# Attention with two problems in one kernel: two heads ahead of the first scores, fewer products in some slots of B, another order of the first loads, a start by quarters, and no branch hint on SyncE

## The chip, the cores and the metric

The kernel runs on one core of a Trainium2 chip. The metric is device time in microseconds (us) of that core. A kernel is run several times, and medians are quoted. Runs are sorted by state: one run of the kernel before took 396.01 us at a granted clock of 0.853 and counts as slow; all others are fast, and only fast runs are compared.

## The reference, cut to what matters

Two independent problems, A and B, of the same form; the outputs stand side by side.

```python
B, Sq, D = 16, 32, 1024
Hq, Hkv, Sk, Dh = 32, 4, 512, 128
q = (x @ wq).reshape(B, Sq, Hq, Dh).transpose(0, 2, 1, 3)
k = jnp.repeat(k_cache, 8, axis=1)
v = jnp.repeat(v_cache, 8, axis=1)
scores = jnp.einsum("bhqd,bhkd->bhqk", q, k) * (Dh ** -0.5)
p = softmax(scores)
o = jnp.einsum("bhqk,bhkd->bhqd", p, v)
out = o.transpose(0, 2, 1, 3).reshape(B, Sq, Hq * Dh) @ wo
# result: concatenate([out_A, out_B], axis=-1), all bfloat16
```

## The kernel before

TensorE (PE in the profile) has three kinds of work: query products (512 tokens at a time, 8 products per head), scores and values of one (batch row, group) pair, and output products. A slot handles one pair: four score products of 256 columns, four value products of the pair five slots earlier, and 6 or 7 "units" taken from one long stream of query and output products of 512 columns. The stream fills PE while ScalarE (ACT) does the exponential and VectorE (DVE) the sums and the normalization. There are 64 slots of A, then 64 of B.

```python
def stream():
    for h in range(REP, HQ):        # REP = 8: heads 8 to 31 of A
        yield from q_units(0, h)
    for h in range(HQ):
        yield from q_units(1, h)
    ...                             # output products of A, then of B
units = stream()
run(units, DC)                      # DC = 8: one head ahead of the first scores
...
for i in range(total_slots + LAG):  # 128 + 5
    if live:
        do_loads(i)
        scores(i)
    run(units, 1)
    ...                             # sums of a group of four slots
    if i >= LAG:
        values(i - LAG)
    ...                             # reciprocals, spread, normalize on DVE
    run(units, 5)
    if live:
        partial_sums(i)
    run(units, 1 - (i % 4 == 3))
```

The first eight heads are a special part. x and the weights arrive in pieces, x is transposed on PE, and dummy products (`warm_up`) keep PE busy meanwhile:

```python
load_x(0, 0, TT // 2)               # all of these loads are issued by SyncE
load_w0(0, 1, 0, NF // 2)
load_x(0, TT // 2, TT)
load_w0(0, 1, NF // 2, NF)
load_w0(1, 2, 0, NF)                # "second row block": weights of rows 128 to 255
load_x(2, 0, TT)
...
load_wq(0, 2, 0, 2)                 # third weight block, first half (heads 8, 9)
load_k(0)
load_wq(0, 2, 2, 4)                 # second half (heads 10, 11)
load_wq(0, 3)
load_k(1)
load_v(0)
load_k(2)
load_wq(0, 4)
load_v(1)
...
warm_up(22)
transpose_x(0, 0, TT // 2)          # two 128-row blocks of x, first half of the tokens
warm_up(3)
first_heads((0, 1), (0,), 0, TT // 2)
transpose_x(0, TT // 2, TT)
first_heads((2,), (0,), 0, TT // 2)
warm_up(1)
first_heads((0, 1, 2), (0,), TT // 2, TT)
first_heads((3, 4, 5), (0,), 0, TT // 2)
first_heads((3, 4, 5), (0,), TT // 2, TT)
first_heads(range(0, NF - 2), (1,)) # the first products of 512 columns
```

At the very end every engine branches over a fallback path that is not taken in these runs. A hint for this branch is given to all five engines. The call stands near the end of the source; in the trace the hints run before the engine's own work, at 0.70 to 0.82 us.

## Time and profile before

| | |
|---|---|
| time before, first three runs | 343.67 us median (343.37 to 343.81) |
| span of the profiled run | 342.1 us (its time: 343.89) |
| PE busy | 338.1 us, 99% |
| first PE instruction, last product starts | 0.93 us, 338.74 us |

These are lines of the page of the kernel before. The first gives the span. The second gives busy time, share and instructions by engine. The third is the chain of work that ended last, by engine. The last two are groups of weight loads (PEld), of the later heads' weights (wq_sb) and of the first heads' (w_sb): after the bars each has busy time and mean, then idle time before it and what ended that.

```profile
span 342.1 us, 5510 instructions
...
PE 338.1 (99%) x2128; PEld 214.6 (63%) x2128; DVE 265.6 (78%) x336; ACT 185.7 (54%) x209; POOL 46.6 (14%) x206
...
PE 99%; ACT 0%; issue 0%; ACTq 0%
...
L301 PEld LDWEIGHTS <-wq_sb 128*128 128x128 bf16 x448 | 43.8, 98 | 31.7 <-DMA wq_sb<-in_A_wq_dram 0.2
...
L533 PEld LDWEIGHTS <-w_sb 128*128 128x128 bf16 x70 | 7.2, 104 | 6.9
```

PE is the whole chain, but busy time of overlapping matmuls doesn't show whether they follow each other as fast as they can. The start-to-start distance of neighbours does. In the instruction records of this run, after 6.5 us, a 512-column product is followed after 216 ns and a 256-column product after 109 ns, whatever comes next. The longest distance is 240 ns, once. So PE never stalls after 6.5 us, and only what lies before can be shortened, apart from the fixed tail after the last product (3.36 us).

This is the timeline of the start of the kernel before: start and length in us, engine, line, operation, output and inputs, count. SPq is SyncE's issue of a DMA.

```profile
0.86 0.45 SPq L465 DMA_DIRECT2D x_sb<-in_A_x_dram  x1
...
0.93 2.52 PE L515 MATMUL q_ps<-const-bfloat16-1.0 128*128 128x128 bf16 x22 [0.93 <-PEq L695]
...
3.29 0.61 PE L523 MATMUL xT_ps<-ident,x_sb 128*128 128x128 bf16 x4
...
3.69 0.53 PE L515 MATMUL q_ps<-const-bfloat16-1.0 128*128 128x128 bf16 x3
...
4.07 0.59 PE L533 MATMUL q_ps<-xT,w_sb 128*128 128x256 bf16 x2
...
5.25 2.58 PE L533 MATMUL q_ps<-xT,w_sb 128*128 128x256 bf16 x13
```

The 22 dummies take 107 ns each, and the 256-column products from 5.41 us on follow each other every 213 ns. At 6.47 us this falls to 110 ns. So PE runs at half rate until then (213 against 110 ns; for 128 columns 107 before and 56 after); I call that moment the switch.

### The profile page before, as it was taken

The page shows a single profiled execution, that of the slowest core. Times are in us where ns is not written, and L with a number is a line of the kernel's source. Part 1 is how long each engine was busy: PE and PEld are TensorE (multiplying, and loading weights), DVE is VectorE, ACT ScalarE, POOL GpSimd, SP SyncE. Part 2 cuts the span into 40 slices and gives each one's busy share as a digit, 9 for nine tenths or more (in the row PEclk, how much of TensorE's full clock was granted, in tenths as well). Part 3 has the DMA queues.
Part 4 walks back from the last instruction along what each step waited for, and adds up shares of the span by engine and source line. Part 5 has one row for each costly group of instructions (what it writes and reads, how often), then busy time and mean ns, then how long its engine had stood idle before and what let it go on. Part 6 is the DMA issues. An engine that isn't in the chain of part 4 may idle for free.

```text
span 342.1 us, 5510 instructions
## 1 busy us (share of the span) xinstructions
PE 338.1 (99%) x2128; PEld 214.6 (63%) x2128; DVE 265.6 (78%) x336; ACT 185.7 (54%) x209; POOL 46.6 (14%) x206
## 2 busy tenths in 40 slices
PE   8999999999999999999999999999999999999996
PEld 7456666666666666666666666666666666666555
DVE  1047988888888889888888888798888888889540
ACT  2067666676666666676655554555454555555110
POOL 0001111101111111111101212222122100111100
DMA  6999999899999998999999856999439996430001
GB/s 194 253 243 183 284 261 256 173 232 269 299 234 248 238 252 231 251 304 303 281 319 259 191 125 180 283 323 211 129 104 306 350 194 139 103 96 17 17 17 33
DMA packets 128093, 71.70 MB, mean 210 GB/s; under 512 B 75840, under 2 KB 127296, under 8 KB 128064
## 3 DMA queue, kind: packets, MB, share of 16 engines
q1 hardware_dynamic: 127536, 70.21, 84.7%
q0 software_dynamic: 384, 1.05, 0.9%
q8 instruction: 17, 0.28, 0.3%
q14 instruction: 12, 0.10, 0.1%
q10 hardware_dynamic: 144, 0.07, 0.1%
HBM read 50.86 MB, written 2.10 MB: 155 GB/s over the span
## 4 chain that ended last, share of the span: by engine, by line
PE 99%; ACT 0%; issue 0%; ACTq 0%
PE f_ps L320 32%; PE q_ps L301 28%; PE ob L425 16%; PE s_ps L357 16%; PE q_ps L533 4%; PE q_ps L515 1%; PE xT_ps L523 0%; ACT o_sb L329 0%; ACTq L329 0%
## 5 line engine op out<-in xcount | busy, mean ns | idle before, releaser
L365 ACT ACTIVATE p_sb<-s_ps,shift 128x1024 bf16<-128x1024 f32 x128 | 142.6, 1114 | 97.8 <-PE s_ps L357 82.0
L376 DVE TRANSPOSE_TENSOR_REDUCE parts<-p_sb 128x32 f32<-128x1024 bf16 x128 | 158.8, 1240 | 19.2 <-ACT p_sb L365 17.6
L320 PE MATMUL f_ps<-wo_sb,oT 128*128 128x512 bf16 (+1 forms) x544 | 131.8, 366 | 0.0
L301 PE MATMUL q_ps<-xT,wq_sb 128*128 128x512 bf16 x448 | 117.4, 379 | 0.0
L425 PE MATMUL ob<-p_sb,v_sb 128*128 128x256 bf16 x512 | 76.8, 273 | 0.0
L357 PE MATMUL s_ps<-qT,kT 128*128 128x256 bf16 x512 | 76.8, 273 | 0.0
L320 PEld LDWEIGHTS <-oT 128*128 128x128 bf16 x544 | 53.2, 98 | 35.8
L357 PEld LDWEIGHTS <-kT 128*128 128x128 bf16 x512 | 56.9, 113 | 28.3
L301 PEld LDWEIGHTS <-wq_sb 128*128 128x128 bf16 x448 | 43.8, 98 | 31.7 <-DMA wq_sb<-in_A_wq_dram 0.2
L425 PEld LDWEIGHTS <-v_sb 128*128 128x128 bf16 x512 | 50.1, 98 | 20.0
L447 DVE TENSOR_TENSOR oT<-r,ob 128x512 bf16<-128x512 f32 x64 | 43.9, 686 | 21.9 <-PE ob L425 20.8
L411 DVE STREAM_TRANSPOSE r<-rall 128x512 f32<-128x512 f32 x64 | 44.2, 691 | 1.1
L309 ACT CAST qT<-q_ps 128x512 bf16<-128x512 f32 x56 | 32.6, 583 | 15.4 <-PE q_ps L301 15.4
L394 POOL COPY half<-cs 64x32 f32<-64x32 f32 x32 | 6.5, 204 | 227.4 <-DVE cs L384 227.3
L329 ACT CAST o_sb<-f_ps 128x512 bf16<-128x512 f32 (+1 forms) x17 | 9.5, 558 | 24.6 <-PE f_ps L320 24.6
L533 PE MATMUL q_ps<-xT,w_sb 128*128 128x512 bf16 (+1 forms) x70 | 15.4, 377 | 0.0
L384 DVE TENSOR_REDUCE cs<-parts 128x32 f32<-128x128 f32 x32 | 12.0, 376 | 1.1
L406 DVE RECIPROCAL rall<-sums 128x32 f32<-128x32 f32 x32 | 10.2, 320 | 3.3 <-POOL sums L403 3.3
L533 PEld LDWEIGHTS <-w_sb 128*128 128x128 bf16 x70 | 7.2, 104 | 6.9
L561 DVE CAST qT<-q_ps 128x512 bf16<-128x512 f32 x4 | 2.5, 683 | 10.2 <-PE q_ps L533 10.2
L331 POOL DMA_DIRECT2D out_dram<-o_sb x8 | 4.6, 574 | 34.7 <-ACT o_sb L329 34.6
L395 POOL TENSOR_TENSOR half<-half,cs 64x32 f32<-64x32 f32 x32 | 7.8, 242 | 2.6
(25 smaller groups left out, 46.3 us busy)
## 6 DMA issues: line engine op xcount, KB each, us to landing
v_sb<-in_A_v_cache_dram SPq DMA_DIRECT2D x16, 512.0 KB, 6.5
wq_sb<-in_B_wq_dram SPq DMA_DIRECT2D x8, 1024.0 KB, 6.0
wo_sb<-in_A_wo_dram SPq DMA_DIRECT2D x8, 1024.0 KB, 6.4
v_sb<-in_B_v_cache_dram SPq DMA_DIRECT2D x16, 512.0 KB, 4.4
wo_sb<-in_B_wo_dram SPq DMA_DIRECT2D x8, 1024.0 KB, 8.4
wq_sb<-in_A_wq_dram SPq DMA_DIRECT2D x5, 1024.0 KB, 6.3
wq_sb<-in_A_wq_dram SPq DMA_DIRECT2D x2, 512.0 KB, 5.8
kT<-in_A_k_cache_dram SPq DMA_TRANSPOSE x64, 4.5
```

The lines of the kernel that those rows point to most:

```text
L301: nc.tensor.matmul(ps[:], lhsT=w[:, dc, (h % 4) * DH:(h % 4 + 1) * DH], rhs=xT[pr][:, dc, :], start=(dc == 0), stop=(dc == DC - 1),)
L309: nc.scalar.copy(out=qT[pr, g][:, :, hl, :], in_=ps[:].rearrange("p (b s) -> p b s", s=SQ),)
L320: nc.tensor.matmul(ps[:, 0:width], lhsT=oT[pr, tt][:, h, :], rhs=wo_tiles[pr, nh, h // REP][:, h % REP, off:off + width], start=(h == 0), ...
L357: nc.tensor.matmul(s_ps[:, c, :], lhsT=kT[:, i % GRP, c, :], rhs=qT[pr, g][:, b, :, :].rearrange("p h s -> p (h s)"), start=True, stop=True,)
L365: nc.scalar.activation(out=p_sb[:], in_=s_ps[:], func=ACTF.Exp, bias=shift[:], scale=SCALE)
L376: nc.vector.tensor_reduce(out=parts[k][:, q, :, :].rearrange("p c h -> p (c h)"), in_=st[i]["p"][:].rearrange("p c (h s) -> p (c h) s", s=SQ),
L384: nc.vector.tensor_reduce(out=cs[:], in_=parts.pop(k)[:].rearrange("p q c h -> p q h c"), axis=AX.X, op=ALU.add,)
L406: nc.vector.reciprocal(out=rall[:, k, :], in_=quad.pop(k)[:])
L411: nc.vector.transpose(out=r[:].rearrange("p n s -> p (n s)"), in_=rall[:, k, o * 2 * REP:(o + 1) * 2 * REP] .unsqueeze(2).to_broadcast([P, ...
L425: nc.tensor.matmul(ob[j][:, q, :], lhsT=v_sb[:, i % GRP, c, :], rhs=st[i]["p"][:, c, :], start=(c == 0), stop=(c == KC - 1),)
L447: nc.vector.tensor_tensor(out=out, in0=rcp.pop(j)[:].rearrange("p (q h) s -> p q h s", h=REP), in1=ob.pop(j)[:].rearrange("p q (h s) -> p ...
L533: nc.tensor.matmul(first_q[h][:, ts], lhsT=w0[dc // HC][:, dc % HC, h * DH:(h + 1) * DH], rhs=xT[0][:, dc, ts], start=(dc == 0 and t0 == 0 ...
```

## The change

Its intent, read from the code: the first real product should come sooner (transpose and copy 128 tokens instead of 256 before it, one dummy less, first DMA issued sooner without SyncE's hint). The first scores and the weights of heads 10 and 11 should have more time to wait for their loads (eight more products ahead of the scores, third weight block whole before K, later weight blocks a slot sooner). The slots of B give the eight products back, so that the tail stays as long. The diff, cut to its core:

```diff
             load_wq(0, 2, 0, 2)
+            load_wq(0, 2, 2, 4)
             load_k(0)
-            load_wq(0, 2, 2, 4)
             load_wq(0, 3)
             load_k(1)
             load_v(0)
+            load_wq(0, 4)
             load_k(2)
-            load_wq(0, 4)
             load_v(1)
 ...
             warm_up(22)
-            transpose_x(0, 0, TT // 2)
-            warm_up(3)
-            first_heads((0, 1), (0,), 0, TT // 2)
-            transpose_x(0, TT // 2, TT)
-            first_heads((2,), (0,), 0, TT // 2)
+            for tt in range(2):
+                transpose_x(0, tt, tt + 1, nc.vector.tensor_copy)
+            transpose_x(1, 0, 2, nc.scalar.copy, spare)
+            warm_up(2)
+            first_heads((0, 1, 2), (0,), 0, 1)
+            transpose_x(0, 2, TT, nc.vector.tensor_copy)
+            transpose_x(1, 2, TT, nc.scalar.copy)
+            first_heads((0, 1, 2), (0,), 1, 2)
             warm_up(1)
 ...            # transpose_x now does one row block; `spare` is one more PSUM buffer
-            run(units, DC)
+            run(units, 2 * DC)
 ...
-                need = ((c4 - 2) * 4 - 1) * DC / 6.75
+                need = ((c4 - 2) * 4 - 2) * DC / 6.75
                 at(max(0, int(need) - 7), load_wq, c4 // 8, c4 % 8)
 ...
-                run(units, 1 - (i % 4 == 3))
+                run(units, i % 4 != 3 and (i < NG or i % 8 != 1))
 ...
-                [nc.sync.engine, nc.scalar.engine, nc.vector.engine, nc.tensor.engine, nc.gpsimd.engine],
+                [nc.scalar.engine, nc.vector.engine, nc.tensor.engine, nc.gpsimd.engine],
```

More of the change, by code (lines that the diff above doesn't have):

```diff
@@ L510, in fast_path @@
                 first_q += [pair_ps[:, k, :] for k in range(2)]
+            spare = psum.tile([P, NTOK], BF16, name="xT_ps", tag="proj")
             first_q += [psum.tile([P, NW], FP32, name="q_ps", tag="proj")[:] for _ in range(2)]
@@ L515, in warm_up, with transpose_x @@
                     nc.tensor.matmul(
-                        first_q[NF - 1][:, 0:P], lhsT=warm, rhs=warm, start=True, stop=True
+                        first_q[HALF][:, 0:P], lhsT=warm, rhs=warm, start=True, stop=True
                     )
-            def transpose_x(d0, t0, t1):
-                for d, copy in ((d0, nc.vector.tensor_copy), (d0 + 1, nc.scalar.copy)):
+            def transpose_x(d, t0, t1, copy, ps=None):
+                if ps is None:
                     ps = psum.tile([P, NTOK], BF16, name="xT_ps", tag="ob")
-                    for tt in range(t0, t1):
-                        nc.tensor.transpose(
-                            ps[:, tt * P:(tt + 1) * P], x_sb[:, tt, d * P:(d + 1) * P], ident[:]
-                        )
-                    ts = slice(t0 * P, t1 * P)
-                    copy(out=xT[0][:, d, ts], in_=ps[:, ts])
+                for tt in range(t0, t1):
+                    nc.tensor.transpose(
+                        ps[:, tt * P:(tt + 1) * P], x_sb[:, tt, d * P:(d + 1) * P], ident[:]
+                    )
+                ts = slice(t0 * P, t1 * P)
+                copy(out=xT[0][:, d, ts], in_=ps[:, ts])
             def first_heads(heads, dcs, t0=0, t1=TT):
@@ L541, in fast_path @@
             warm_up(22)
-            transpose_x(0, 0, TT // 2)
-            warm_up(3)
-            first_heads((0, 1), (0,), 0, TT // 2)
-            transpose_x(0, TT // 2, TT)
-            first_heads((2,), (0,), 0, TT // 2)
+            for tt in range(2):
[6 more added lines that the diff above has]
+            first_heads((0, 1, 2), (0,), 1, 2)
             warm_up(1)
-            first_heads((0, 1, 2), (0,), TT // 2, TT)
-            first_heads((3, 4, 5), (0,), 0, TT // 2)
-            first_heads((3, 4, 5), (0,), TT // 2, TT)
+            first_heads((0, 1, 2), (0,), 2, TT)
+            first_heads((3, 4, 5), (0,), 0, 2)
+            first_heads((3, 4, 5), (0,), 2, TT)
             first_heads(range(0, NF - 2), (1,))
-            transpose_x(2, 0, TT)
+            transpose_x(2, 0, TT, nc.vector.tensor_copy)
+            transpose_x(3, 0, TT, nc.scalar.copy)
             first_heads(range(NF - 2, NF), (1,))
```

## The prediction

> **What bounds the kernel.** TensorE, almost without a gap. The page has PE busy 338.1 of 342.1 us (99%), and the chain of waits that ended last is 99% PE. By start-to-start distances in the instruction records: after about 6.5 us 512-column products follow each other every 216 ns and 256-column ones every 109 ns, whatever comes between, with no longer gap up to the end (the longest is 240 ns, once). The 92 products after the last values are as dense. The list of waits names PE once, 0.9 us, before its first instruction; one wait of a weight load for a DMA (0.2 us) stayed hidden. Reordering the steady part can win nothing.
>
> What is not dense is the ends: 0.93 us before PE starts, then 22 dummy products, then a slow clock. Until 6.47 us the distances are 107 ns for 128 columns and 213 ns for 256; then 110 for 256. [...] the trace agrees with the two rates (107 and 56 ns for 128 columns), and places the switch 5.5 us after PE's first instruction. The last 2.5 us are the last copy and output DMA.
>
> **What the change does.**
> 1. Start: one dummy less (107 ns at the slow clock), the first token half transposed, copied and multiplied by quarters. The first real product waited until 4.07 us; a 128-column copy should be done by about 3.80 us (256-column copies took 0.29, 512-column 0.42, so I estimate 0.22) and the two dummies end at about 3.88, so no wait. Counting 39 slow steps of 107 ns instead of 40, and waits of together about 0.08 us gone, the products of the second token half start near 5.06 instead of 5.25 us. If the clock switches at the same moment, that 0.19 us is worth half afterwards: about 0.1 us.
> 2. No hint on SyncE: its hint took 60 ns plus issue, so the first DMA issues about 0.08 us earlier (0.86 before). x landed at 3.24, just when PE wanted it. At the end its branch may take longer, but it has from 336.4 to 341.1 us to spare.
> 3. Two heads ahead (8 more products before the first scores, so these come near 23.0 instead of 21.3 us), whole third weight block before K: K's first slice lands about 3 us later (18.0 before) but is wanted 1.7 later: still about 2 us early. The block's second half (landed 23.15, wanted about 23.3) and the fifth block (38.3, wanted about 38) gain 2 to 3 us of margin. PE did not stall there before: safety, not time.
> 4. Nine products fewer in slots of B: it balances the eight ahead; the tail has 93 instead of 92. VectorE needs about 8.4 us per four slots against 9.1 us in the shortened groups: still room.
>
> PE's work in columns is the same but for the dummy. Sum: 343.67 - 0.1, perhaps 0.2 with earlier data. I predict **343.5 us**, 343.0 to 344.0. Faster by over 2%: 0.5%; within 2%: 99%; slower: 0.5%.
>
> **In the profile:** first scores near 23.0 us; distances unchanged at 216/109 ns; the second token half's first product near 5.06 us; slow clock until about 6.5 us; the last matmul at about 338.9; no new PE waits.
>
> **What would make it wrong:** [...] a stall at K or V because the transposing DMAs come later; VectorE falling behind in the shortened slots; SyncE's unhinted branch outlasting the last output.

Two passages are cut out because no trace or run shows them: where the half rate comes from, with how long it lasts and how much it scatters, and the first of the risks, that the clock switches at another moment, with a size for it. "The two rates" are the measured 107 and 56 ns that stand beside them. 343.67 less 0.1 is 343.57, less 0.2 is 343.47, so 343.5.

## The result, and the profile after

| | median us | range | runs |
|---|---|---|---|
| before | 343.56 | 343.37 to 343.95 | 6 |
| after | 343.33 | 343.06 to 343.81 | 6 |

The ratio is 0.9993, with a 95% interval of 0.998 to 1.0006. A ratio is the mean time of one kernel's fast runs over that of the other's of the same rounds, so it is not quite the ratio of the medians quoted. The measured time lies within the predicted range. The times alone don't show that the change helps at all, since the interval contains 1. The traces do, and they show something that I had not predicted.

The page of the changed kernel, the same lines:

```profile
span 341.5 us, 5512 instructions
...
PE 337.4 (99%) x2130; PEld 214.4 (63%) x2130; DVE 265.6 (78%) x337; ACT 185.8 (54%) x209; POOL 46.7 (14%) x206
...
PE 99%; ACT 0%; issue 0%; ACTq 0%
...
L301 PEld LDWEIGHTS <-wq_sb 128*128 128x128 bf16 x448 | 43.8, 98 | 32.2
...
L534 PEld LDWEIGHTS <-w_sb 128*128 128x128 bf16 x73 | 7.1, 102 | 6.8 <-DMA w_sb<-in_A_wq_dram 0.3
```

And the timeline of its start:

```profile
0.74 0.45 SPq L465 DMA_DIRECT2D x_sb<-in_A_x_dram  x1
...
3.24 0.63 PE L524 MATMUL xT_ps<-ident,x_sb 128*128 128x128 bf16 x4
...
3.67 0.42 PE L516 MATMUL q_ps<-const-bfloat16-1.0 128*128 128x128 bf16 x2
...
3.88 0.53 PE L534 MATMUL q_ps<-xT,w_sb 128*128 128x128 bf16 x3
...
5.00 2.19 PE L534 MATMUL q_ps<-xT,w_sb 128*128 128x256 bf16 x13
...
6.15 0.55 PEld L534 LDWEIGHTS <-w_sb 128*128 128x128 bf16 x4 [0.28 <-DMA w_sb<-in_A_wq_dram]
...
22.60 0.60 PE L357 MATMUL s_ps<-qT,kT 128*128 128x256 bf16 x4
```

The first DMA is issued 0.12 us sooner (0.74 for 0.86). The first real product starts at 3.88 instead of 4.07 us. But the span fell by 0.64 us, three times what these could give, and a new wait stands at 6.15 us. The switch explains both. Here the trace has a record of the granted clock, which rises at 4.89 us, where the run before switched at 6.47. With the faster clock, PE reached the products of the second row block ("first wide product" below: 512 columns) before their weights had landed (6.10 us). The distance to the first of them was 277 instead of 109 ns, a wait of 0.17 us. So two profiled runs with two different switches cannot tell what the change did. The experiments must hold the switch apart from the change.

### The profile page after: what moved, and what is told of

It reads as the page before. It is cut to its first block, busy times and chain, and to the rows that moved or that the text cites. A ratio compares the mean times of both kernels' runs of the same rounds, so it can differ in the third digit from the quotient of the medians.

```text
span 341.5 us, 5512 instructions
## 1 busy us (share of the span) xinstructions
PE 337.4 (99%) x2130; PEld 214.4 (63%) x2130; DVE 265.6 (78%) x337; ACT 185.8 (54%) x209; POOL 46.7 (14%) x206
## 4 chain that ended last, share of the span: by engine, by line
PE 99%; ACT 0%; issue 0%; ACTq 0%
PE f_ps L320 32%; PE q_ps L301 28%; PE ob L425 16%; PE s_ps L357 16%; PE q_ps L534 4%; PE q_ps L516 1%; PE xT_ps L524 0%; ACT o_sb L329 0%; ACTq L329 0%
## 5 line engine op out<-in xcount | busy, mean ns | idle before, releaser
L534 PE MATMUL q_ps<-xT,w_sb 128*128 128x512 bf16 (+2 forms) x73 | 14.9, 359 | 0.0
```

The lines of the kernel that those rows point to most:

```text
L534: nc.tensor.matmul(first_q[h][:, ts], lhsT=w0[dc // HC][:, dc % HC, h * DH:(h + 1) * DH], rhs=xT[0][:, dc, ts], start=(dc == 0 and t0 == 0 ...
```

## The experiments

Theory A: the steady part takes the same time in both kernels; the moment of the switch is chance; the change gains about 0.1 us in the start. Rivals: the change itself brings the switch forward (B), the gain comes from the new order (C), or the dummies don't matter to the switch (D). Unless the edit says otherwise, the base is the changed kernel. All twelve runs gave correct results. Each call has its own runs of the kernel before on the same chip: their medians were 343.54 us in the first call (343.52 without its slow run) with the repeat, the start alone, the order alone and no dummies, 343.87 in the second (the two delayed kernels, no compensation, two queues), 343.58 in the third (no hint, 20 dummies, one load on ScalarE) and 343.74 in the last (hint back). In some traces some 40 of 2130 PE records are missing; a distance of twice the usual length with nothing named as waited for is such a hole, not a stall.

### The same kernel again

No edit.

> The changed kernel, unaltered. The two profiles differ by 0.64 us in span (342.10 and 341.47), but the TensorE clock switched at 6.47 us in the one before and at 4.89 us in the one after. Theory A (the moment of the switch is chance, each us of it is worth half a us, the change itself is worth 0.1 us): over the repeats the spans scatter over 0.5 us or more, and a profile that switches later is longer by half the delay, apart from 0.17 us of DMA wait that only the early switch shows. Rival B (the change itself brings the switch forward, or shortens the steady part): every repeat switches near 4.9 us and has a span of 341.4 to 341.5. Median 343.2 to 343.6 under A, 343.2 to 343.3 under B.

Measured: 343.33 us (343.08 to 343.95), ratio 0.9993 (0.9977 to 1.0008). The profiled run switched at 5.53 us, not 4.89, and its span was 341.58 us. So the kernel doesn't fix the switch, and B as stated falls. Whether the start shifts the odds of an early switch is taken up below the table at the end. The six times fall into two groups: four from 343.08 to 343.37, two at 343.93 and 343.95.

### The start alone, and the order alone

The first is the kernel before with the new first part (quarters, two dummies) and without SyncE's hint. The second is the kernel before with the other hunks (loads, `2 * DC`, `need`, slots of B).

> The kernel before with the quartered start and without the SyncE hint; order and slots of before. Theory A (all of the gain lies in the start): the median is 0.1 to 0.2 us under that of before, the first product of the second token half near 5.0 us, distances of 216 and 109 ns afterwards. Rival C (the gain comes from the new order of products and loads): as before within 0.05 us. The difference is near the noise, so the trace decides: 39 slow steps in place of 40 and no waits before 5.0 us.

> The kernel before with only the order changed: two heads ahead, fewer products in the slots of B, third weight block whole before K, weight loads a slot sooner; start and SyncE hint of before. Theory A: PE was gapless there, so no change: median within 0.1 us of before, start distances as before, first scores near 23 us. Rival C: 0.2 us or more faster.

Measured: the start alone 343.50 us (343.21 to 344.62), the order alone 343.78 (343.40 to 344.10), before in the same call 343.54. Ratios to before: 0.9991 (0.9977 to 1.0005) and 0.9998 (0.9985 to 1.0012). None is clear of 1. By the medians theory A missed in both: the start alone is 0.02 to 0.04 us under before, not 0.1 to 0.2, which is what C expected, and the order alone is 0.24 to 0.26 above, not within 0.1 (C, which wanted it 0.2 faster, missed there). The expectation had left the decision to the trace. Of the runs, the start alone has its fastest at 343.21, 343.22 and 343.25; the six fastest of before lie at 343.46 to 343.54. The order alone has its fastest at 343.40. That comparison was chosen after the runs; it speaks for A and against C, and so do the traces: the order alone keeps the old start distances and takes as long from its first wide product to its last product as the kernel before (331.94 us).

In the trace of the start alone, the distances up to 5.05 us are 107 ns throughout. The first product of the second token half starts there (5.05), as in the repeat, against 5.25 in the kernel before. But its profiled run was its slowest, 344.62 us. The list of its weight loads' waits (us in total, times, longest) says why:

```profile
PEld L301 <- DMA wq_sb<-in_A_wq_dram: 0.9, 2, 0.6
...
PEld L534 <- DMA w_sb<-in_A_wq_dram: 0.6, 1, 0.6
PEld L425 <- DMA v_sb<-in_A_v_cache_dram: 0.5, 1, 0.5
```

With the old order the second half of the third weight block landed at 24.34 us in this run (23.15 in the kernel before's profile) and PE stood: the distance at 23.77 us is 620 instead of 216 ns, so 0.40 us were lost, 0.32 at the first values that need the second load of V (41.1 us), 0.28 at row-block weights (7.9 us). The last of these stalls has nothing to do with the change of order, since both kernels issue those loads in the same order. The other 0.72 us show that the old order can stall without any added delay; this is the one trace that shows it.

### Does the order buy margin?

To both kernels, one load of 256 KB that nothing reads was added, so that what follows lands later:

```diff
             load_wq(0, 2, 0, 2)
+            extra = blk_tile([P, REP * DH], "extra")
+            nc.sync.dma_start(out=extra[:], in_=wq_v[:, 0, 0:REP * DH])
```

> The kernel before with one more load, 256 KB that nothing reads, right behind the first half of the third weight block, so that everything behind it lands about 1.0 to 1.5 us later (an estimate from the 3.1 us that 512 KB took there). Theory E (the new order buys margin at the third weight block, not time): in the kernel before, the second half of the block landed at 23.15 us and was wanted at about 23.2, so nearly all of the delay becomes a wait of PE: 0.8 to 1.6 us longer than before, seen as a wait of the weight load near 23.3 us. Rival F (margins are ample in both orders, the order is worth nothing): within 0.2 us of before.

> The changed kernel with the same extra 256 KB load in the same place. Theory E: the third block landed at 19.1 us and its second half is wanted near 22.9, the first slice of K at 19.6 and is wanted at 22.4, the fourth block at 26.1 and is wanted near 27.4; a delay of 1.0 to 1.5 us uses this up but no more: 0 to 0.3 us longer than the changed kernel, so 343.2 to 343.7 us, and about 1 us faster than the other kernel with the same load. Rival F: both kernels with the load differ by no more than 0.2 us.

Measured in one call: 344.81 us (344.02 to 345.30) for the old order and 343.88 (343.71 to 344.24) for the new one; before without the load 343.87. Ratios to before: 1.002 (1.0001 to 1.0039) and 0.9998 (0.9981 to 1.0015). The difference of the two medians is 0.93 us, as theory E expected. Not all of it is the order, since the two kernels differ in the start too: in the profiled runs the first wide product starts at 6.92 and 6.60 us, and the time from there to the last product differs by 0.82 us (332.76 and 331.94). The new order landed somewhat above the range I gave it (343.2 to 343.7); the reason comes below. The waits of the weight loads, first the old order:

```profile
PEld L517 <- issue: 0.9, 1, 0.9
PEld L301 <- DMA wq_sb<-in_A_wq_dram: 0.8, 1, 0.8
PEld L425 <- DMA v_sb<-in_A_v_cache_dram: 0.4, 1, 0.4
```

and the new order, which has none for a DMA:

```profile
PEld L518 <- issue: 0.9, 1, 0.9
```

In the old order the half block landed at 24.80 us, and PE's distances of 829 and 400 ns (216 undisturbed) make 0.80 us of stall. In the new order it landed at 20.10 us. So margin is what the order buys, about 0.8 us under this delay, shown by a delay made on purpose.

Both kernels of this pair pay something else, equally. Their tails, from the last product's start to the end, are 3.79 us instead of 3.36. In the records of the changed kernel, the DMAs of SyncE and ScalarE take semaphores 102 to 109 in turn, and at the end SyncE waits for these eight in the same order; those that it finds done follow each other after 0.06 us (336.21, 336.27, 336.33, 336.39, 336.45 us for 102 to 106). The last output has 109 and landed at 340.49; the wait for it, at 340.51, is the last. In the delayed new order, with one DMA more, seven more waits follow the last output's landing (340.95 to 341.37 us). It is the same in both, so the comparison holds, but it explains most of why the delayed new order is above the changed kernel (0.43 of 0.55 us, between two calls).

### The dummies

```diff
-            warm_up(22)
...
-            warm_up(2)
...
-            warm_up(1)
```

> The changed kernel with all 25 dummy products taken out. Theory A ([...] the dummies buy an early switch): PE starts near 3.05 us when x lands instead of 0.93; the real products start some 0.2 us earlier, but the switch comes about 2 us later, so the median is 0.5 to 1.2 us longer than that of the changed kernel and the switch lies between 6.5 and 9 us. Rival D (the switch comes at a fixed time after launch whatever PE does): the switch stays between 4.9 and 6.5 us and the kernel is as fast or 0.1 to 0.2 us faster.

Measured: 344.66 us (344.09 to 344.96), against 343.33 for the changed kernel in the same call: 1.33 longer, a little more than expected; ratio to before 1.0025 (1.001 to 1.0041). PE started at 2.95 us and the switch came at 8.07, beyond every switch seen with dummies and an undisturbed start (3.77 to 6.73). D falls: dummies buy an earlier switch. PE's wait list shows the idle start:

```profile
PE xT_ps L524 <- DMA x_sb<-in_A_x_dram: 2.9, 1, 2.9
```

### The slots of B without the compensation

```diff
-                run(units, i % 4 != 3 and (i < NG or i % 8 != 1))
+                run(units, i % 4 != 3)
```

> The changed kernel without the nine products fewer in the slots of B. Theory A (PE is gapless, so where its products stand does not matter): same as the changed kernel within 0.1 us; the last values come some 2 us earlier and the tail has 9 products fewer (84 in place of 93). Rival G (the thinner slots of B are needed, because VectorE or a PSUM buffer falls behind, or the thinner slots themselves cost): 0.3 us or more slower or faster, with waits or longer distances in B.

Measured: 344.28 us (344.05 to 344.81), ratio to before 1.0011 (0.9994 to 1.0028), before in the same call 343.87. Theory A failed in this expectation, and so did my sign: the last values come later (327.23 us against 324.53), as the products that were in the tail now stand ahead of them. This is the timeline near the end:

```profile
323.24 0.38 PE L320 MATMUL f_ps<-wo_sb,oT 128*128 128x512 bf16 x1
323.44 0.69 DVE L447 TENSOR_TENSOR oT<-r,ob 128x512 bf16<-128x512 f32 x1 [0.63 <-PE ob L425]
...
324.19 1.47 PE L320 MATMUL f_ps<-wo_sb,oT 128*128 128x512 bf16 x6 [0.57 <-DVE oT L447]
...
327.86 0.69 DVE L447 TENSOR_TENSOR oT<-r,ob 128x512 bf16<-128x512 f32 x1 [2.99 <-PE ob L425]
...
328.60 1.41 PEld L320 LDWEIGHTS <-oT 128*128 128x128 bf16 x8 [0.41 <-DVE scratch L659]
```

The stream has run ahead. It asks for output products of the last 128 tokens while DVE is still normalizing them. The distances at 323.24 and 328.31 us are 945 and 299 ns, so PE stalls 0.73 and 0.08 us. (The last line names the DVE instruction at 328.50 us as the releaser; the normalization before it, which writes the oT that PE reads, ended at 328.55.) "Where the products stand does not matter" holds only as long as what they read is ready. The nine products fewer are what makes the eight ahead free.

### The hint

Two kernels: no hint on any engine, and the hint on SyncE put back.

> The changed kernel with the branch hint taken from all engines, not from SyncE alone. In the profile of the changed kernel SyncE issued its first DMA at 0.74 us (0.86 with its hint), and its branch at the end went on after 0.19 us, as with the hint (0.20). Theory H (a hint costs some 0.1 us at the start and saves nothing at the end here): PE starts near 0.85 us and ScalarE's branch at the end (339.27 to 339.75 in the changed kernel) takes no longer; 0 to 0.1 us faster than the changed kernel. Rival I (the hint hides a fetch at the end, and only SyncE's did not matter because it waits anyway): ScalarE, whose branch stands 0.65 us before the last DMA is done, comes 1 us or more later and the kernel is 0.3 to 2 us slower.

Measured: 345.05 us (344.65 to 345.39), ratio to before 1.0039 (1.0025 to 1.0052), clearly slower. The instruction records at the end, in us:

```
                    ScalarE branches   ScalarE goes on   SyncE branches   SyncE goes on
before, all hints   339.90             340.39            336.38           336.59
changed kernel      339.27             339.75            335.75           335.94
no hint at all      339.75             342.33            336.23           336.41
```

ScalarE's branch took 2.59 us without its hint and 0.48 with it. SyncE's took 0.19 without (in both lower rows) and 0.20 with. Rival I holds for ScalarE: while it stands at its branch without a hint, instructions are transferred. These are the DMA transfers of instructions from 339.8 to 342.3 us of this run (count, MB, share of 16 engines), while ScalarE stands:

```profile
q8 instruction: 1, 0.02, 3.0%
q14 instruction: 1, 0.01, 1.0%
```

The first is of 16 KB and lasts from 340.87 to 342.09 us; ScalarE goes on at 342.33. While ScalarE stands at its branch in the changed kernel (339.27 to 339.75) there is none, and none while SyncE stands at its branch without a hint. Why SyncE's branch is as short without its hint is not shown. At the start PE began at 0.78 us instead of 0.93, a gain that the end loses many times over.

> The changed kernel with the hint on SyncE put back. Profiles of the changed kernel and of dummies_20 have the same span (341.47 and 341.46) although the clock switched at 4.89 and 3.77 us: in both PE then waits for the weights of the second row block, which land at 6.10 us. Theory J (in runs with an early switch this landing is the floor, and leaving out the hint moved it 0.11 us forward): with the hint back the first DMA issues at 0.86 us, these weights land near 6.2 us, and the fastest runs lie near 343.35 to 343.4 us in place of 343.06 to 343.35. Rival K (the hint is worth nothing, the early floor comes from the quarters): fastest runs as the changed kernel's, 343.1 to 343.3. The median depends on how many runs switch late and tells little.

Measured: 343.61 us (343.52 to 343.96), ratio to before 0.9998 (0.9984 to 1.0011). No run is under 343.5, where the changed kernel had nine of twelve under 343.4. But those ran in other calls, and the fastest here lie 0.12 us above the range that J gave them, so the times alone are weak. The landings carry the reading: in the four profiled runs with SyncE's hint (before, order alone, delayed old order, this one) the weights of the second row block landed at 6.21 to 6.30 us, in the eight without it and with all first loads on SyncE at 5.97 to 6.19; the means are 6.25 and 6.08. Theory J holds; K falls. In this run they landed at 6.29 us, and PE waited for them in the timeline, 0.18 us later than in the changed kernel (6.15), after a switch at 5.01 us. The first line below runs on into the wide products:

```profile
5.06 2.31 PE L534 MATMUL q_ps<-xT,w_sb 128*128 128x256 bf16 x13
...
6.33 0.55 PEld L534 LDWEIGHTS <-w_sb 128*128 128x128 bf16 x4 [0.40 <-DMA w_sb<-in_A_wq_dram]
```

### Tries at a better start

20 dummies in place of 22:

> The changed kernel with 20 dummies ahead of the first transpose in place of 22. x landed at 3.01 us in the changed kernel's profile and the first transpose ran at 3.24, bound by the dummies. Theory A: the real products start up to 0.21 us sooner at the slow clock, so a late switch gains 0.1 us and an early one less, because the weights of the second row block land near 6.1 us anyway: 343.2 to 343.4, not to be told from the changed kernel. Rival (x often lands later than in that profile): waits of PE before the first transpose and no gain or 0.1 us loss.

Measured: 343.53 us (343.25 to 343.89), ratio to before 1.0 (0.9986 to 1.0013): somewhat above the range that I gave (343.2 to 343.4), and not to be told from the changed kernel. Its profile is the best evidence for the floor: the switch came at 3.77 us, 1.1 us before that of the changed kernel's, the products got 0.34 us ahead (the last of the first row block started at 5.53 instead of 5.87 us), and all of it was lost at the same landing:

```profile
5.72 1.36 SPq L471 DMA_TRANSPOSE xT<-in_A_x_dram  x1
6.14 0.55 PEld L534 LDWEIGHTS <-w_sb 128*128 128x128 bf16 x4 [0.62 <-DMA w_sb<-in_A_wq_dram]
6.14 0.82 PE L534 MATMUL q_ps<-xT,w_sb 128*128 128x512 bf16 x3 [0.34 <-DMA w_sb<-in_A_wq_dram]
```

So I tried to make these weights land sooner, with a second queue: three weight loads at the head of ScalarE's program (with 20 dummies), then only the one that matters.

```diff
+            load_w0(0, 1, 0, NF // 2, nc.scalar)      # two_queues: these three
+            load_w0(0, 1, NF // 2, NF, nc.scalar)
+            load_w0(1, 2, 0, NF, nc.scalar)           # act_late: this one, after the next line
             nc.scalar.preload_act_table_set("natural_log_exp_and_others")
```

> The changed kernel with the first three loads of the first weights issued by ScalarE, beside those of x on SyncE, and 20 dummies in place of 22. In the changed kernel's profile PE waited 0.17 us at 5.9 to 6.1 us for the weights of the second row block, which were issued fifth by one queue at 0.5 us each and landed at 6.10. If the issue rate of one queue is what limits the start after an early switch, these weights land before 5.2 us, the wait is gone and the start of the real products moves 0.2 us forward: 0.1 to 0.3 us faster than the changed kernel (343.0 to 343.2). If the DMA engines' own rate limits it, they land near 6.0 us as before and nothing is won.

> The changed kernel with only the load of the second row block's first weights moved to ScalarE's queue, behind its table load (issued near 2.1 us instead of 2.73). With three loads moved to the very start, x landed 0.8 us later and the kernel lost. If that loss was the contention of the first loads, this later issue leaves x at 3.0 us, lands these weights before 5.9 us and takes the 0.17 us wait of an early switch away: 0 to 0.2 us faster than the changed kernel. If a second queue beside the first costs by itself, x(0) is undisturbed but the third and fourth loads land later and PE waits before 5.5 us: same or slower.

Measured: 344.57 us (344.11 to 346.17), ratio 1.0026 (1.0003 to 1.0048), and 346.00 (345.55 to 346.39), ratio 1.0065 (1.0052 to 1.0079). Both lose. With three loads the first piece of x landed at 3.79 instead of 3.01 us and the weights in question at 6.98 instead of 6.10. With one load the assumption failed: the issue did not wait for the table load and stood at 0.85 us. The weights landed at 4.28, but x at 4.48. PE then stood 1.1 us, and the switch came at 10.42 us:

```profile
PE xT_ps L524 <- DMA x_sb<-in_A_x_dram: 1.1, 1, 1.1
```

With three loads moved, the weights in question were issued at 1.75 instead of 2.73 us and landed 0.88 us later, and x, wanted first, 0.78 us later. With one load of 192 KB moved, its weights landed 1.82 us sooner, and x 1.47 us later than the 3.01 of the changed kernel. In both, PE then stood for x (0.6 and 1.1 us). No version that beats the changed kernel came of this.

## Why the prediction was right

One table holds most of it. All times are from traces, in us. "Switch" is the record of the granted clock (for the kernel before, the fall of the distances). "First wide" is the start of the first 512-column product, which needs the weights of the second row block. "Steady" is from there to the start of the last product.

| profiled run | switch | those weights landed | first wide | steady | time |
|---|---|---|---|---|---|
| before | 6.47 | 6.21 | 6.80 | 331.94 | 343.89 |
| order alone | 6.66 | 6.30 | 6.89 | 331.94 | 344.10 |
| hint back | 5.01 | 6.29 | 6.33 | 331.95 | 343.55 |
| after | 4.89 | 6.10 | 6.15 | 331.96 | 343.26 |
| after again | 5.53 | 5.97 | 6.27 | 331.94 | 343.37 |
| 20 dummies | 3.77 | 6.10 | 6.14 | 331.95 | 343.25 |
| start alone | 5.79 | 6.09 | 6.40 | 332.97 (stalls) | 344.62 |
| uncompensated | 5.32 | 6.09 | 6.17 | 332.78 (stalls) | 344.10 |
| delayed new order | 6.20 | 6.06 | 6.60 | 331.94 | 344.23 |
| delayed old order | 6.73 | 6.21 | 6.92 | 332.76 (stalls) | 345.27 |

Is the switch chance? The three profiled runs with the old start switched at 6.47 to 6.73 us, later than the nine with the new start, dummies and no halt of PE over 0.6 us in it (3.77 to 6.39). In all twelve it came 2.8 to 5.8 us after PE's first product, a spread of 3 us. One thing speaks against a cause in the start, and it is worked out, not seen directly: 17 of the 39 fast runs of the kernel before in the four calls have spans of 341.5 to 341.7 us. Less 331.94 and the tail of 3.36, this puts their first wide product at 6.2 to 6.4, which the table shows for no switch later than 5.8. So by this estimate the old start, too, switches early in many runs.

Point by point:

- "Reordering the steady part can win nothing": right. Old and new order take 331.94 to 331.96 us when nothing stalls. The 216 ns per product leave no room.
- "PE did not stall there before: safety, not time": right for the run that I had, and the delayed pair shows the safety (0.82 us of its 0.93). In the profiles of before and after, the third block's second half landed at 19.13 instead of 23.15 us and the fifth block at 34.14 instead of 38.27: 4 us sooner, where I had expected 2 to 3 us of margin. "PE did not stall" was too strong for all runs: the start alone, with the old order, stalled by 1.0 us in its profiled run, 0.72 of it at the two loads for which the new order leaves more time. Of the 45 fast runs of the kernel before, 7 took over 344.2 us; of 28 runs of kernels with the new order and no other disturbance (after, its repeat, order alone, hint back, 20 dummies), none did. I chose the 344.2 after seeing the runs, and a stall is shown only in the one profiled, so this is likely rather than shown.
- "it balances the eight ahead; the tail has 93 instead of 92": right, and needed. Without it PE stalls 0.81 us near the end. I had costed VectorE per group of slots, not the readiness of the last tokens, which is where it would have failed.
- Start by quarters, 39 slow steps instead of 40, second token half at 5.06 instead of 5.25 us: right where the slow clock lasts that long (5.05 us in the repeat and in the start alone). "Worth half afterwards" also stands as arithmetic, but only if the switch comes late, and the 0.19 was too large: in the kernel before, the product at 5.25 had waited and was followed after 167 instead of 213 ns, so the next one starts at 5.41 against 5.27, and at 5.39 in the order alone. An estimate of the worth from the table: each us by which the switch comes later costs 0.49 us (1 - 109/213), so with a switch at 6.47 the first wide product of the delayed new order would start at 6.74, against 6.80 in the kernel before. That is 0.06 us, not 0.1.
- The step that was most mis-sized: SyncE's hint, which I put at 0.08 us and treated as a possible extra, because "x landed at 3.24, just when PE wanted it". The first DMA came 0.12 us sooner. What it moves is not only x but every load behind it, among them the weights of the second row block (issued at 2.73 instead of 2.84 us). In the three profiled runs with a switch by 5.01 us PE ended up waiting for those. Putting the hint back moved their landing from 6.10 to 6.29 us and the first wide product from 6.15 to 6.33: 0.18 us, the same as the difference of the two spans (341.65 and 341.47). The three fastest runs with the hint back (343.52, 343.55, 343.61) are no better than the three fastest of the kernel before in the same call (343.35, 343.50, 343.72). So the quarters seem to give nothing there, as the products they hurry wait at the same landing; no run of the kernel before with an early switch was profiled to show it.
- "slow clock until about 6.5 us" and "no new PE waits": wrong for the profiled run, for the reason that I had named as a risk, the clock's switch (cut from the text above). That one was 1.6 us earlier; the first wide product came only 0.65 us sooner, the change's own share included, since the loads then set the pace. The first scores came at 22.60 us, not near 23.0.

So the predicted total fits (0.1 to 0.2 us; medians differ by 0.23, not clear of the scatter), partly by luck: one part was too large, the other too small, and the mechanism was half of it. By the traces the gain is the hint in runs with an early switch (0.18 us), the quarters in runs with a late one (0.06), and, likely, fewer stalls in the rare late loads.

What stays open: what sets the moment of the switch; what share of runs switches early, since only profiled runs show it; and why the stalls of the old order occur in some runs only.

## What to carry to other kernels

Where an engine is gapless, as PE was here (216 ns from one 512-column product to the next), a reordering can be worth its safety margin alone, so measure it with a delay made on purpose, not with medians. When the start hangs on a clock whose switch differs from run to run, as here (3.77 to 6.73 us), find the two floors (clock-bound and load-bound), and ask of each part of a change which floor it lowers. Products could be moved ahead for free here only until they overtook what they read (0.81 us of stalls without the nine fewer).
